# A gated FFT and token-MLP mixer: half-line tables with even samples first, ScalarE evictions that put the samples back in order, and x's first two row groups loaded whole

## The chip, the cores and the metric

The kernel runs on one core of one Trainium2 chip. The metric is device time in microseconds (us) of one execution; the median of several runs is compared. A profile is one execution taken by the hardware profiler; its span goes from the first to the last instruction. The engines are TensorE (PE, with its weight loads listed as PEld), VectorE (DVE), ScalarE (ACT), GpSimd (POOL) and SyncE (SP), which here only issues DMAs.

## The reference

Two mixers of the same shape are blended by a gate. S = 2048 tokens, D = 512 channels, F = 1792 hidden units; everything is bf16.

```python
def reference(A_x, A_w_r, A_w_i, B_x, B_w1, B_b1, B_w2, B_b2, gate_w):
    x = A_x
    g = sigmoid((x * gate_w).sum(-1, keepdims=True))
    # A: 2-D real FFT over (S, D), product with a complex W[S, 257], inverse
    X = rfft2(x, axes=(-2, -1)) * (A_w_r + 1j * A_w_i)
    a = irfft2(X, s=(S, D), axes=(-2, -1)).astype(bfloat16)
    # B: layer norm over D, then an MLP across the tokens
    h = layernorm(x)
    u = gelu(einsum("bsd,sf->bdf", h, B_w1) + B_b1)
    b = (einsum("bdf,fs->bds", u, B_w2) + B_b2).transpose(0, 2, 1)
    return g * a + (1 - g) * b
```

Both branches get the same x.

## The kernel before

**Tiling.** The 2048 rows of x are split as (q a r): q in 0..3, a in 0..127 on the partitions, r in 0..3. So there are 16 row groups j = 4q + r of 128 rows. Row group 0 is (q 0, r 0); the groups are loaded in the order of `Q0 = (0, 2, 1, 3)` for r = 0.

**The MLP branch.** The statistics of a row group are taken by DVE (L487, L488), for two groups by ACT (L491, L495); ACT takes a square root (L511), DVE the reciprocal (L516), and DVE (L521) or ACT (L527) writes the normalized `h`. The first product, `m1` (L705), is 14 blocks of F times 16 row groups: 224 matmuls of 512 columns. ACT applies the gelu (L721). The second product, `m2` (L1008), is another 224 matmuls of 512 columns; ACT evicts it scaled by 1 - g (L1014), for the last pair of row groups DVE does (L1021).

**The FFT branch.** It is done by butterflies on DVE and matmuls with tables of cosines and sines on PE:

- forward, along the tokens: a four-point butterfly on DVE (L535 to L542) for each r, then four matmul groups `fa` (L554 to L557) with table `ta`, each evicted by ACT (L560);
- a radix-4 step across the r (L585 to L601), then the transform along the channels, `fb` (L653, table `tb`, evicted at L660);
- the product with W: the mirrored half of W is made on PE by a matrix `flip` (L757; its last column, number 256, at L767 and L770); `wprep` (L777 to L781) scales row 0 of W by one half and takes sums and differences of columns 0 and 256; `nyq` (L801 to L804) does the line of the Nyquist frequency; `c0a`, `c0b`, `c0c` (L846) do column 0 apart;
- inverse along the tokens: `i1` (L890 for odd r, L895 to L898 for even r, table `ti`), evicted by `i1ev` (L904, L906), and DVE butterflies `zf` and `fq` (L914 to L927);
- inverse along the channels: `i3` (L967 to L970, table `tg`), evicted by ACT with the gate as scale at `i3ev` (L974), then DVE butterflies `es` (L987 to L993) and the sum of both branches (L1027).

The channels of a row are split by parity, h = 0 and 1; each half line has 256 time samples, and `i3` makes of the spectrum two parts: a part even in the sample number (129 values, by cosines) and a part odd in it (127 values, by sines). They stand side by side as 129 + 127 columns of one PSUM row. `es` then adds and subtracts them to get samples and mirrored samples. The terms of frequency 0 and of the line's last frequency share row 0 of the tables.

**The order of the work.** Nothing is scheduled by hand. Each piece is a task (`add`) with an engine, an estimated duration, what it reads and writes, a priority and the PSUM buffers it takes and frees. A small planner (`Plan.order`) simulates the engines with these durations and writes the tasks out in the order in which they start; `rate` gives it the speed of DMAs and `mm` the time of matmuls, with a least time of 120 columns. The order on each engine is then fixed. PSUM has four banks `acc`, two `fa` and two `fb`; during the first `m1` blocks one `fa` bank holds the output of block 0, so that one is left for the forward groups.

**The loads.** All loads go out on SP's queue but a few at the start: ACT's queue carries half of each of the first two row groups of x and the first two loads of w1. The halves are 64 partitions each (L366 to L370).

The functions that the change touches, with the line numbers of the profile:

Of the kernel before, what the change touches and what calls it, by code (L numbers as in the profile page):

```python
# [16 lines left out]
P = 128  # L17
# [17 lines left out]
def make_tables():  # L35
# [10 lines left out]
    for r in range(4):  # L46
        s = 4 * p + r
        for n, k0 in enumerate((0, 2)):
            th = ang(s, k0 + 4 * np.arange(64), S)
            ta[:, r, n * 128:n * 128 + 64] = np.cos(th)  # L50
            ta[:, r, n * 128 + 64:n * 128 + 128] = -np.sin(th)
        ta[:, r, 64] = alt
        th = ang(s, 1 + 4 * (p ^ 96), S)
        ta[:, r, 256:384] = np.cos(th)
        ta[:, r, 384:512] = -np.sin(th)
        ta[:, r, 512:640] = -np.cos(th)

        k = np.where(p < 64, 4 * p, 2 + 4 * (p - 64))
        o, w = ti_at(r)
        v = ti[:, o:o + w]  # L60
        if r % 2:
            sg = np.where(p < 64, 1.0, -1.0)[:, None]
            th = ang(k, s, S)
            v = v.reshape(P, 7, P)
            v[:, 0] = np.cos(th)
            v[:, 1] = sg * np.cos(th)
            v[:, 2] = -np.sin(th)
            v[:, 3] = -sg * np.sin(th)
            v[0, 2:4] = alt * (0.5 ** 0.5 if r == 1 else -(0.5 ** 0.5))
            th = ang(1 + 4 * (p ^ 96), s, S)  # L70
            v[:, 4] = -np.sin(th)
            v[:, 5] = np.cos(th)
            v[:, 6] = np.sin(th)
            ti[:, o:o + w] = v.reshape(P, w)
        else:
            s5 = np.append(s, 512)
            for lt, kk in enumerate((k, 1 + 4 * (p ^ 96))):
                th = ang(kk, s5, S)
                c, n = np.cos(th), -np.sin(th)
                if lt == 0:  # L80
                    n[0, 0:P] = 0.0 if r == 0 else -alt
                u = v[:, 256 * lt:256 * lt + 256]
                u[:, 0:P], u[:, P:] = c[:, 0:P], n[:, 0:P]
                if r == 0:
                    u[:, P] = c[:, P] if lt == 0 else -n[:, P]
    ti[:, 2945:3072] = ti[:, 129:256]
    ti[0, 2816:2945] = np.append(alt, 1.0)
# [12 lines left out]
    for r in range(4):  # L100
        cf[m[0, 0], r, 0] = 1.0
        cf[8, r, 0] = (1.0, -1.0)[r % 2]
        cf[m[1, r % 2], r, 0] = (1.0, -1.0, -1.0, 1.0)[r]
        if r != 2:
            cf[m[2, 0], r, 1], cf[m[3, 0], r, 1] = 1.0, (1.0, -1.0)[r % 2]
        if r != 0:
            cf[m[2, 1], r, 1], cf[m[3, 1], r, 1] = (0.0, -1.0, 1.0, 1.0)[r], (0.0, -1.0, -1.0, 1.0)[r]
    tb = np.concatenate([tb.reshape(P, 768), cf.reshape(P, 8)], 1)

    tg = np.zeros((P, 642))  # L110
    sc = 2.0 / (D * S)
    d = np.arange(129)
    for h in range(2):
        th = ang(2 * p + h, d, D)
        c, n = sc * np.cos(th), -sc * np.sin(th)
        if h == 0:
            c[0], n[0] = sc / 2, 0.0
            tg[:, 513:642], tg[:, 129:256] = c, n[:, 1:128]
        else:
            tg[:, 256:384], tg[:, 384], tg[:, 385:512] = c[:, 0:128], -n[:, 128], n[:, 1:128]  # L120
    tg[0, 0:129] = np.where(d % 2 == 0, 1.0, -1.0) * sc / 2
    return {"flip": bf(np.eye(P)[::-1]), "ta": bf(ta), "ti": bf(ti), "tb": bf(tb), "tg": bf(tg)}


def rate(at):
    return 260e3 if at < 8.4 else 388e3


class Task:
# [117 lines left out]
def d1(n):  # L247
    return 0.07 + n / 960.0
# [4 lines left out]


def mm(*ns):
    return sum(max(n, 120) / 2400.0 + 0.0025 for n in ns)

# [7 lines left out]
def kernel(  # L265
# [192 lines left out]
    def ld_ti():  # L458
        t["ti"] = sb([P, 3072], BF16, "rot")
        dma(t["ti"][:], tabs["ti"])  # L460
    load("tg", [P, 642], BF16, tabs["tg"], 164352, prio=39.5)


    def xe(r):
# [297 lines left out]
                add("ACT", act(512), wfe, reads=[("pw", comp, lt, a)], writes=[("W~", comp, lt)], prio=3, free=[tag])  # L762

    def wfn():
        pw = t["pwn"] = ps([P, 4, 2], F32, "fa", 2)
        for e in range(4):
            T.matmul(pw[:, e], lhsT=t["flip"][:], rhs=t["wt"][:, :, 3 - e, 256], start=True, stop=True)  # L767
    add("PE", mm(*[4] * 4), wfn, reads=[("wt", 0), ("wt", 1), "flip"], writes=["pwn"], prio=5, alloc=["fa"])
    wtk = [("W~", comp, 0) for comp in range(2)]
    add("ACT", 0.3, lambda: A.copy(t["W"][:, :, 0, :, 1, 256], t["pwn"][:].rearrange("p e k -> p k e")),  # L770
        reads=["pwn"], writes=wtk, prio=3, free=["fa"])
# [10 lines left out]
    add("DVE", 0.8, wprep, reads=[], writes=[("W", 0), ("W", 1), "wpm"] + wtk, prio=1)  # L782


    for lt in range(2):
# [8 lines left out]
        if lt == 0:  # L794
            def nyq():
# [77 lines left out]
    for rs, h in ((0, 0), (0, 1), (1, 0), (1, 1)):  # L873
        for r in (rs, rs + 2):
            for lt in range(2):
                tag = ("fa", "fb")[lt]

                def i1(h=h, r=r, lt=lt, tag=tag):
# [6 lines left out]
                    for v in range(2):  # L885
# [71 lines left out]
    for p in range(NJ // 2):  # L957
# [4 lines left out]
        def i3(j0=j0, j1=j1, rs=rs):  # L962
            g = t["tg"]
            for n, j in enumerate((j0, j1)):
                p3 = t["i3", j] = ps([P, 2, L], F32, ("fa", "fb")[n], 2)
                zv = [xph(h)[:, 2048 * rs:2048 * rs + 2048].rearrange("p (q v r a) -> p q v r a", q=4, v=2, r=2)[:, j // 4, :, n, :] for h in range(2)]
                T.matmul(p3[:, 0], lhsT=zv[0][:, 1], rhs=g[:, 0:256], start=True, stop=False)  # L967
                T.matmul(p3[:, 0, 0:129], lhsT=zv[0][:, 0], rhs=g[:, 513:642], start=False, stop=True)
                T.matmul(p3[:, 1, 0:128], lhsT=zv[1][:, 0], rhs=g[:, 256:384], start=True, stop=True)
                T.matmul(p3[:, 1, 128:256], lhsT=zv[1][:, 1], rhs=g[:, 384:512], start=True, stop=True)  # L970
        add("PE", mm(*[128] * 6, 256, 256), i3, reads=[("z", rs, 0), ("z", rs, 1), "tg"], writes=[("i3", j0), ("i3", j1)], prio=4, alloc=["fa", "fb"])
# [104 lines left out]
```

## Time and profile before

| | us |
|---|---|
| median of 3 runs | 127.93 (127.70 to 128.27) |
| the profiled execution | 128.01 |
| its span | 126.2 |
| PE busy | 121.4 (96%) |
| DVE busy | 114.4 (91%) |
| ACT busy | 81.0 (64%) |
| first matmul of `m1` starts | 5.74 |
| last eviction (L1021) starts | 123.46 |

How to read it: busy times of PE come from modelled ends, and records overlap; the distance from one start to the next is what a matmul costs. About 13 of the 756 matmuls have no record, each of which leaves a hole of 0.216 us. The first ten matmuls (L356) work on zeros and warm the clock; they start 0.427 us apart, the later ones of the same size 0.216.

### The profile page before, as it was taken

The page shows a single profiled execution, that of the slowest core. Times are in us where ns is not written, and L with a number is a line of the kernel's source. Part 1 is how long each engine was busy: PE and PEld are TensorE (multiplying, and loading weights), DVE is VectorE, ACT ScalarE, POOL GpSimd, SP SyncE. Part 2 cuts the span into 40 slices and gives each one's busy share as a digit, 9 for nine tenths or more (in the row PEclk, how much of TensorE's full clock was granted, in tenths as well). Part 3 has the DMA queues.
Part 4 walks back from the last instruction along what each step waited for, and adds up shares of the span by engine and source line. Part 5 has one row for each costly group of instructions (what it writes and reads, how often), then busy time and mean ns, then how long its engine had stood idle before and what let it go on. Part 6 is the DMA issues. An engine that isn't in the chain of part 4 may idle for free.

```text
span 126.2 us, 2141 instructions
## 1 busy us (share of the span) xinstructions
PE 121.4 (96%) x743; PEld 68.9 (55%) x756; DVE 114.4 (91%) x273; ACT 81.0 (64%) x165; POOL 0.2 (0%) x4
## 2 busy tenths in 40 slices
PE   6999999999999999999999999999999999999991
PEld 2244555555655466654455555555577767655590
DVE  2599999999999999999999999999988999999951
ACT  0972689699999999999520004732299999952200
POOL 0000000000000000000000000000000000000000
PEclk9999999999999999999999999999999999999999
DMA  2999999996367964599999940000000000021751
GB/s 63 266 368 363 379 363 362 349 330 89 99 124 225 275 133 112 125 393 412 413 408 409 407 173 0 0 5 0 3 0 0 0 5 0 0 82 58 280 208 44
DMA packets 18220, 23.12 MB, mean 183 GB/s; under 512 B 2191, under 2 KB 15905, under 8 KB 18209
## 3 DMA queue, kind: packets, MB, share of 16 engines
q1 hardware_dynamic: 17616, 22.36, 53.3%
q10 hardware_dynamic: 592, 0.62, 2.0%
q8 instruction: 6, 0.10, 0.3%
q14 instruction: 6, 0.04, 0.1%
HBM read 20.86 MB, written 2.10 MB: 182 GB/s over the span
## 4 chain that ended last, share of the span: by engine, by line
PE 93%; DMA 3%; ACTq 1%; issue 1%; DVE 0%
PE acc L1008 32%; PE acc L705 30%; PE fb L705 5%; PE fb L1008 5%; PE fa L705 3%; DMA wa<-in_B_w_dram 3%; PE fa L554 2%; PE fb L653 2%; PE fa L653 2%; PE fa L890 2%; PE fb L890 1%; PE fa L555 1%; ACTq L306 1%; PE fa L557 1%; PE fa L556 1%
## 5 line engine op out<-in xcount | busy, mean ns | idle before, releaser
L705 PE MATMUL acc<-h,wb 128*128 128x512 bf16 x108 | 25.9, 379 | 0.1
L1008 PE MATMUL acc<-gl,wb 128*128 128x512 bf16 (+1 forms) x94 | 24.0, 371 | 0.2
L1008 PE MATMUL acc<-gl,wa 128*128 128x512 bf16 (+1 forms) x97 | 23.8, 371 | 0.1
L1014 ACT ACTIVATE x<-acc,ombb,omg 128x512 bf16<-128x512 f32 x12 | 9.1, 782 | 21.2 <-PE acc L1008 21.2
L1008 PEld LDWEIGHTS <-wa 128*128 128x128 bf16 x126 | 13.5, 113 | 9.9
L1008 PEld LDWEIGHTS <-wb 128*128 128x128 bf16 x126 | 13.3, 113 | 9.3
L705 PE MATMUL acc<-h,wa 128*128 128x512 bf16 x62 | 17.5, 382 | 0.1
L705 PEld LDWEIGHTS <-wb 128*128 128x128 bf16 x112 | 10.7, 98 | 10.5
L705 PEld LDWEIGHTS <-wa 128*128 128x128 bf16 x112 | 10.3, 98 | 10.7 <-DMA wa<-in_B_w_dram 1.0
L487 DVE BATCH_NORM_STATS2 stats<-x 128x6 f32<-128x512 bf16 x14 | 9.5, 678 | 2.5 <-DMA x<-in_A_x_dram 2.5
L560 ACT CAST xp<-fa 128x512 bf16<-128x512 f32 x16 | 9.1, 582 | 2.0 <-PE fa L557 2.0
L735 ACT ACTIVATE x<-x 128x512 bf16<-128x512 bf16 x16 | 10.2, 691 | 0.0
L721 ACT ACTIVATE gl<-acc,b1f 128x512 bf16<-128x512 f32 x11 | 7.9, 718 | 3.2 <-PE acc L705 3.2
L705 PE MATMUL fb<-h,wa 128*128 128x512 bf16 x31 | 9.5, 379 | 0.1
L527 ACT ACTIVATE h<-x,nmr,rstd 128x512 bf16<-128x512 bf16 x11 | 8.4, 807 | 1.1 <-DMA wb<-in_B_w_dram 0.8
L705 PE MATMUL fa<-h,wa 128*128 128x512 bf16 x16 | 6.1, 393 | 0.1
L653 PEld LDWEIGHTS <-X 128*128 128x128 bf16 x64 | 4.7, 98 | 2.1
L974 ACT ACTIVATE B<-fb,g 128x512 bf16<-128x512 f32 x8 | 5.7, 713 | 0.0
L974 ACT ACTIVATE B<-fa,g 128x512 bf16<-128x512 f32 x8 | 5.6, 706 | 0.1
L356 PE MATMUL fa<-xp 128*128 128x512 bf16 x10 | 4.4, 631 | 1.2 <-DVE xp L317 1.2
L660 ACT CAST X<-fb 128x512 bf16<-128x512 f32 x8 | 5.1, 636 | 0.0
L511 ACT ACTIVATE rstd<-mv,eps 128x1 f32<-128x1 f32 (+1 forms) x11 | 3.2, 293 | 2.9 <-DVE mv L488 2.4
(169 smaller groups left out, 234.6 us busy)
## 6 DMA issues: line engine op xcount, KB each, us to landing
wb<-in_B_w_dram SPq DMA_DIRECT2D x11, 512.0 KB
wa<-in_B_w_dram SPq DMA_DIRECT2D x7, 512.0 KB
wa<-in_B_w_dram SPq DMA_DIRECT2D x2, 896.0 KB
wb<-in_B_w_dram SPq DMA_DIRECT2D x4, 384.0 KB
out_dram<-x SPq DMA_DIRECT2D x3, 512.0 KB
x<-in_A_x_dram SPq DMA_DIRECT2D x2, 512.0 KB
wa<-in_B_w_dram SPq DMA_DIRECT2D x2, 448.0 KB
rot<-dft_ti SPq DMA_DIRECT2D x1, 768.0 KB
```

The costliest lines, as they stand in the source:

```text
L356: T.matmul(pw[:], lhsT=t["warm"][:, 0:P], rhs=t["warm"], start=True, stop=True)
L487: V.bn_stats(out=t["stats"][:, j, :], in_=t["x"][:, j // 4, j % 4, :])
L527: add("ACT", 0.71, lambda j=j: A.activation(t["h"][:, j // 4, j % 4, :], t["x"][:, j // 4, j % 4, :], ActF.Identity, bias=t["nmr"][:, j:j ...
L560: add("ACT", act(512), lambda r=r, dq=dq: A.copy(xe(r)[:, :, :, dq, :], t["pa", r, dq][:]), reads=[("pa", r, dq)], writes=[("X", r, dq)], ...
L653: T.matmul(pb[:, k % 2, k // 2], lhsT=t["X"][:, lt, EX[e], c, k, :], rhs=tbl(k, c), start=True, stop=True)
L660: A.copy(t["X"][:, lt, EX[e]].rearrange("p c j l -> p (c j l)").rearrange("p (h c g b) -> p h c g b", h=2, c=2, b=2)[:, :, c], t["pb", lt, ...
L705: T.matmul(t["u", ft][:], lhsT=w[:, j // 4, j % 4, c * P:(c + 1) * P], rhs=t["h"][:, j // 4, j % 4, :], start=(j == jorder[0]), stop=(j == ...
L721: gelus.append(add("ACT", act(512, 1) , lambda ft=ft: A.activation(t["gl"][:, ft, :], t["u", ft][:], ActF.Gelu_apprx_tanh, bias=t["b1f"][: ...
L735: A.activation(t["x"][:, q, r, :], t["x"][:, q, r, :], ActF.Copy, accum_out=t["glog"][:, 4 * q + r:4 * q + r + 1])
L974: A.activation(eo_v(p)[:, n], t["i3", j][:], ActF.Copy, scale=t["g"][:, j:j + 1])
L1008: T.matmul(t["y", j, m][:, cs], lhsT=w[:, o, 512 * q + r:512 * q + 512:4], rhs=t["gl"][:, ft, cs], start=(ft == 0), stop=(ft == NFT - 1))
L1014: A.activation(tbuf(j).rearrange("p h d -> p (h d)"), t["y", j, 0][:], ActF.Identity, bias=t["ombb2"][:, j:j + 1], scale=t["omg"][:, j:j + 1])
```

## The change

Five edits in one.

1. **Tables and matmuls of `i3`, and of `i1` for r = 0, lt = 0.** The columns of the half-line tables are sorted by the parity of the sample number, even ones first. The cosine of a frequency and of its complement agree at even samples and differ in sign at odd ones, and so the row that the two end frequencies share is arranged anew: instead of one matmul of 256 columns and one of 129, there are three of 191, 64 and 65 columns. The second input half (`zv[1]`) keeps two matmuls of 128 columns, each now written as two runs of 64.
2. **The evictions put the samples back in order.** `i3ev` and, for r = 0 and lt = 0, `i1ev` read PSUM in order and write SBUF with a step of two elements. What follows on DVE is unchanged.
3. **Sums and differences of the end columns.** With the shared row holding sum and difference of the two end frequencies, the scaling of row 0 of W goes (its factors move to the tables), `c0c` adds and subtracts in place of a copy, `nyq` gets an addition and a subtraction, and a table for the lines on partition 0 is changed to match.
4. **The flip of column 256** is one matmul of 8 columns in place of four of 2.
5. **Loads and costs.** Row groups (q 0, r 0) and (q 2, r 0) of x are loaded whole, the first on SP's queue, the second on ACT's. The planner's DMA rate at the start goes from 260 to 275 KB/us and the least time of a matmul from 120 to 62 columns; the costs of the changed tasks follow.

The order which the planner writes is therefore another one in places. On SP and ACT one DMA is gone at the start; the four groups `fa` of r = 0 stand after 24, 28, 32 and 38 matmuls of `m1` (before: 25, 28, 32 and 37).

```diff
 def rate(at):
-    return 260e3 if at < 8.4 else 388e3
+    return 275e3 if at < 8.4 else 388e3
...
 def mm(*ns):
-    return sum(max(n, 120) / 2400.0 + 0.0025 for n in ns)
+    return sum(max(n, 62) / 2400.0 + 0.0025 for n in ns)
...
     for q in (0, 2):
-        for n in range(2):
-            hp = slice(n * P // 2, (n + 1) * P // 2)
-            ld([("xh", q, n)], lambda hp=hp, q=q: t["x"][hp, q, 0, :], x4[hp, q, 0, :], 65536, -9.5 + 0.1 * q, ("SP", "ACT")[n])
-        add("DVE", 0.0, lambda: None, reads=[("xh", q, 0), ("xh", q, 1)], writes=[("x", 0, q)], prio=-9)
+        ld([("x", 0, q)], lambda q=q: t["x"][:, q, 0, :], x4[:, q, 0, :], 131072, -9.5 + 0.1 * q, "ACT" if q else "SP")
...
-        pw = t["pwn"] = ps([P, 4, 2], F32, "fa", 2)
-        for e in range(4):
-            T.matmul(pw[:, e], lhsT=t["flip"][:], rhs=t["wt"][:, :, 3 - e, 256], start=True, stop=True)
+        pw = t["pwn"] = ps([P, 2, 4], F32, "fa", 2)
+        T.matmul(pw[:], lhsT=t["flip"][:], rhs=t["wt"][:, :, :, 256], start=True, stop=True)
...
-        V.tensor_scalar_mul(W[0:1, :, 0, 0, :, 0:257], W[0:1, :, 0, 0, :, 0:257], 0.5)
...
-                V.tensor_mul(nn[:, :, 0], t["c0"][0:1, 0, 0, 1, :], wn[:, 0, 0:257:256])
+                V.tensor_mul(pz[:, 0:2], t["c0"][0:1, 0, 0, 1, :], wn[:, 0, 0:257:256])
+                V.tensor_add(nn[:, 0, 0:1], pz[:, 0:1], pz[:, 1:2])
+                V.tensor_sub(nn[:, 1, 0:1], pz[:, 0:1], pz[:, 1:2])
...
-            V.tensor_copy(t["B"][:, lt, :, :, 0], t["ce"][:, lt].rearrange("p e c k -> p e (c k)"))
+            b, ce = t["B"][:, lt], t["ce"][:, lt]
+            V.tensor_add(b[:, :, 0:4:2, 0], ce[:, :, :, 0], ce[:, :, :, 1])
+            V.tensor_sub(b[:, :, 1:4:2, 0], ce[:, :, :, 0], ce[:, :, :, 1])
...
-                            if n > P:
-                                T.matmul(p1[:, v], lhsT=d(1), rhs=t["ti"][:, 2816:3072], start=True, stop=False)
...
+                            if r == 0 and lt == 0:
+                                T.matmul(p1[:, v, 65:256], lhsT=d(1), rhs=t["ti"][:, 2816:3007], start=True, stop=False)
+                                T.matmul(p1[:, v, 128:192], lhsT=d(0), rhs=u[:, 66:130], start=False, stop=True)
+                                T.matmul(p1[:, v, 0:65], lhsT=d(0), rhs=u[:, 0:65], start=True, stop=True)
...
-                        A.copy(t["ze"][:, h, r // 2, lt], t["i1", h, r, lt][:])
+                        o, i = t["ze"][:, h, r // 2, lt], t["i1", h, r, lt][:]
+                        if r == 0 and lt == 0:
+                            o, i = o.rearrange("p v (n w) -> p v w n", w=2), i.rearrange("p v (w n) -> p v w n", w=2)
+                        A.copy(o, i)
...
-                T.matmul(p3[:, 0], lhsT=zv[0][:, 1], rhs=g[:, 0:256], start=True, stop=False)
-                T.matmul(p3[:, 0, 0:129], lhsT=zv[0][:, 0], rhs=g[:, 513:642], start=False, stop=True)
-                T.matmul(p3[:, 1, 0:128], lhsT=zv[1][:, 0], rhs=g[:, 256:384], start=True, stop=True)
-                T.matmul(p3[:, 1, 128:256], lhsT=zv[1][:, 1], rhs=g[:, 384:512], start=True, stop=True)
+                ph = p3[:, 1].rearrange("p (w n) -> p w n", w=2)
+                gh = g[:, 322:578].rearrange("p (c w n) -> p c w n", c=2, w=2)
+                T.matmul(p3[:, 0, 65:256], lhsT=zv[0][:, 1], rhs=g[:, 0:191], start=True, stop=False)
+                T.matmul(p3[:, 0, 128:192], lhsT=zv[0][:, 0], rhs=g[:, 258:322], start=False, stop=True)
+                T.matmul(p3[:, 0, 0:65], lhsT=zv[0][:, 0], rhs=g[:, 192:257], start=True, stop=True)
+                for c in range(2):
+                    T.matmul(ph[:, :, 64 * c:64 * c + 64], lhsT=zv[1][:, c], rhs=gh[:, c], start=True, stop=True)
...
-                A.activation(eo_v(p)[:, n], t["i3", j][:], ActF.Copy, scale=t["g"][:, j:j + 1])
+                A.activation(eo_v(p)[:, n].rearrange("p h (n w) -> p h w n", w=2), t["i3", j][:].rearrange("p h (w n) -> p h w n", w=2), ActF.Copy, scale=t["g"][:, j:j + 1])
```

More of the change, by code (lines that the diff above doesn't have):

```diff
@@ L83, in make_tables @@
                 u[:, 0:P], u[:, P:] = c[:, 0:P], n[:, 0:P]
[L84 to L87, printed above, removed]
+                if r == 0 and lt:
+                    u[:, P] = -n[:, P]
+                elif r == 0:
+                    ti[:, 2816:2879], ti[:, 2943:3007] = n[:, 2:P:2], n[:, 1:P:2]
+                    u[:, 0:65], u[:, 66:130] = c[:, 0:129:2], c[:, 1:P:2]
+                    u[0, 66:130], ti[0, 2879:2943] = 0.0, 1.0
     tb = np.zeros((P, 2, 2, 3, 64))
@@ L107, in make_tables @@
             cf[m[2, 1], r, 1], cf[m[3, 1], r, 1] = (0.0, -1.0, 1.0, 1.0)[r], (0.0, -1.0, -1.0, 1.0)[r]
+    cf[:, 0] = cf[:, 0] @ np.array([[1.0, 1.0], [1.0, -1.0]])
+    cf[0:2] *= 0.5
     tb = np.concatenate([tb.reshape(P, 768), cf.reshape(P, 8)], 1)
-    tg = np.zeros((P, 642))
+    tg = np.zeros((P, 578))
     sc = 2.0 / (D * S)
@@ L116, in make_tables @@
         if h == 0:
-            c[0], n[0] = sc / 2, 0.0
-            tg[:, 513:642], tg[:, 129:256] = c, n[:, 1:128]
-        else:
-            tg[:, 256:384], tg[:, 384], tg[:, 385:512] = c[:, 0:128], -n[:, 128], n[:, 1:128]
-    tg[0, 0:129] = np.where(d % 2 == 0, 1.0, -1.0) * sc / 2
+            tg[:, 0:63], tg[:, 127:191] = n[:, 2:128:2], n[:, 1:128:2]
+            tg[:, 192:257], tg[:, 258:322] = c[:, 0:129:2], c[:, 1:128:2]
+            tg[0] = 0.0
+            tg[0, 63:127] = tg[0, 192:257] = sc / 2
+        else:
+            tg[:, 322:386], tg[:, 386:450] = c[:, 0:128:2], c[:, 1:128:2]
+            tg[:, 450], tg[:, 451:514], tg[:, 514:578] = -n[:, 128], n[:, 2:128:2], n[:, 1:128:2]
     return {"flip": bf(np.eye(P)[::-1]), "ta": bf(ta), "ti": bf(ti), "tb": bf(tb), "tg": bf(tg)}
 def rate(at):
-    return 260e3 if at < 8.4 else 388e3
+    return 275e3 if at < 8.4 else 388e3
 class Task:
@@ L460, in ld_ti @@
         dma(t["ti"][:], tabs["ti"])
-    load("tg", [P, 642], BF16, tabs["tg"], 164352, prio=39.5)
+    load("tg", [P, 578], BF16, tabs["tg"], 147968, prio=39.5)
     def xe(r):
@@ L764, in wfn @@
     def wfn():
-        pw = t["pwn"] = ps([P, 4, 2], F32, "fa", 2)
-        for e in range(4):
-            T.matmul(pw[:, e], lhsT=t["flip"][:], rhs=t["wt"][:, :, 3 - e, 256], start=True, stop=True)
-    add("PE", mm(*[4] * 4), wfn, reads=[("wt", 0), ("wt", 1), "flip"], writes=["pwn"], prio=5, alloc=["fa"])
+        pw = t["pwn"] = ps([P, 2, 4], F32, "fa", 2)
+        T.matmul(pw[:], lhsT=t["flip"][:], rhs=t["wt"][:, :, :, 256], start=True, stop=True)
+    add("PE", mm(8), wfn, reads=[("wt", 0), ("wt", 1), "flip"], writes=["pwn"], prio=5, alloc=["fa"])
     wtk = [("W~", comp, 0) for comp in range(2)]
-    add("ACT", 0.3, lambda: A.copy(t["W"][:, :, 0, :, 1, 256], t["pwn"][:].rearrange("p e k -> p k e")),
+    add("ACT", 0.3, lambda: A.copy(t["W"][:, :, 0, :, 1, 256], t["pwn"][:, :, ::-1]),
         reads=["pwn"], writes=wtk, prio=3, free=["fa"])
@@ L781, in wprep @@
         V.tensor_sub(pv[1], ends[1][:, :, 0], ends[1][:, :, 1])
-    add("DVE", 0.8, wprep, reads=[], writes=[("W", 0), ("W", 1), "wpm"] + wtk, prio=1)
+    add("DVE", 0.4, wprep, reads=[], writes=[("W", 0), ("W", 1), "wpm"] + wtk, prio=1)
     for lt in range(2):
@@ L803, in nyq @@
                 V.tensor_add(nn[:, 1], na[:, 1, 1], na[:, 0, 0])
-                V.tensor_mul(nn[:, :, 0], t["c0"][0:1, 0, 0, 1, :], wn[:, 0, 0:257:256])
-            add("DVE", 3 * d1(512) + 0.1, nyq, reads=[("B", i, e) for i in range(2) for e in range(4)] + [("W", 0), ("W", 1), ("c0", 0)] + pbk, writes=["nn"], prio=0.5)
+                V.tensor_mul(pz[:, 0:2], t["c0"][0:1, 0, 0, 1, :], wn[:, 0, 0:257:256])
+                V.tensor_add(nn[:, 0, 0:1], pz[:, 0:1], pz[:, 1:2])
+                V.tensor_sub(nn[:, 1, 0:1], pz[:, 0:1], pz[:, 1:2])
+            add("DVE", 3 * d1(512) + 0.35, nyq, reads=[("B", i, e) for i in range(2) for e in range(4)] + [("W", 0), ("W", 1), ("c0", 0)] + pbk, writes=["nn"], prio=0.5)
         def c0b(lt=lt):
@@ L845, in c0c @@
         def c0c(lt=lt):
-            V.tensor_copy(t["B"][:, lt, :, :, 0], t["ce"][:, lt].rearrange("p e c k -> p e (c k)"))
-        add("DVE", 0.15, c0c, reads=[("ce", lt)], writes=bk, prio=pr)
+            b, ce = t["B"][:, lt], t["ce"][:, lt]
+            V.tensor_add(b[:, :, 0:4:2, 0], ce[:, :, :, 0], ce[:, :, :, 1])
+            V.tensor_sub(b[:, :, 1:4:2, 0], ce[:, :, :, 0], ce[:, :, :, 1])
+        add("DVE", 0.3, c0c, reads=[("ce", lt)], writes=bk, prio=pr)
         if lt == 0:
@@ L891, in i1 @@
                         else:
-                            n = 129 if r == 0 and lt == 0 else P
                             u = ti[:, 256 * lt:256 * lt + 256]
-                            if n > P:
-                                T.matmul(p1[:, v], lhsT=d(1), rhs=t["ti"][:, 2816:3072], start=True, stop=False)
-                            else:
-                                T.matmul(p1[:, v, n:], lhsT=d(1), rhs=u[:, n:], start=True, stop=True)
-                            T.matmul(p1[:, v, 0:n], lhsT=d(0), rhs=u[:, 0:n], start=(n == P), stop=True)
-                i1t[h, r, lt] = add("PE", mm(*([256] * 4 if r % 2 else [128] * 4)), i1, reads=[("T", lt, r % 2), "ti"] + ([("T", lt, 1)] if r == 2 else []), writes=[("i1", h, r, lt)], prio=3, alloc=[tag])
+                            if r == 0 and lt == 0:
+                                T.matmul(p1[:, v, 65:256], lhsT=d(1), rhs=t["ti"][:, 2816:3007], start=True, stop=False)
+                                T.matmul(p1[:, v, 128:192], lhsT=d(0), rhs=u[:, 66:130], start=False, stop=True)
+                                T.matmul(p1[:, v, 0:65], lhsT=d(0), rhs=u[:, 0:65], start=True, stop=True)
+                            else:
+                                T.matmul(p1[:, v, P:], lhsT=d(1), rhs=u[:, P:], start=True, stop=True)
+                                T.matmul(p1[:, v, 0:P], lhsT=d(0), rhs=u[:, 0:P], start=True, stop=True)
+                i1t[h, r, lt] = add("PE", mm(*([256] * 4 if r % 2 else [128] * 4 if r or lt else [191, 64, 65] * 2)), i1, reads=[("T", lt, r % 2), "ti"] + ([("T", lt, 1)] if r == 2 else []), writes=[("i1", h, r, lt)], prio=3, alloc=[tag])
                 def i1ev(h=h, r=r, lt=lt):
@@ L966, in i3 @@
                 zv = [xph(h)[:, 2048 * rs:2048 * rs + 2048].rearrange("p (q v r a) -> p q v r a", q=4, v=2, r=2)[:, j // 4, :, n, :] for h in range(2)]
[L967 to L971, printed above, removed]
+                ph = p3[:, 1].rearrange("p (w n) -> p w n", w=2)
[5 more added lines that the diff above has]
+                    T.matmul(ph[:, :, 64 * c:64 * c + 64], lhsT=zv[1][:, c], rhs=gh[:, c], start=True, stop=True)
+        add("PE", mm(*[191, 64, 65, 128, 128] * 2), i3, reads=[("z", rs, 0), ("z", rs, 1), "tg"], writes=[("i3", j0), ("i3", j1)], prio=4, alloc=["fa", "fb"])
         for n, j in enumerate((j0, j1)):
             def i3ev(j=j, n=n, p=p):
-                A.activation(eo_v(p)[:, n], t["i3", j][:], ActF.Copy, scale=t["g"][:, j:j + 1])
+                A.activation(eo_v(p)[:, n].rearrange("p h (n w) -> p h w n", w=2), t["i3", j][:].rearrange("p h (w n) -> p h w n", w=2), ActF.Copy, scale=t["g"][:, j:j + 1])
             add("ACT", act(512, 1), i3ev, reads=[("i3", j), "g"] + ([("eo", j0)] if n else []), writes=[("eo", j)], prio=1.5, free=[("fa", "fb")[n]],
```

## The prediction

> **What bounds the kernel now.** I read the page's first two parts, then its chain of waits, then the timeline of the first 8 us and of the stage of the last transform. Busy shares and slices of TensorE (PE):
>
> ```profile
> PE 121.4 (96%) x743; PEld 68.9 (55%) x756; DVE 114.4 (91%) x273; ACT 81.0 (64%) x165; POOL 0.2 (0%) x4
> PE   6999999999999999999999999999999999999991
> PE 93%; DMA 3%; ACTq 1%; issue 1%; DVE 0%
> ```
>
> The reader should see that PE has no hole and that 93% of the chain is PE. So the end is: when PE starts its real work, plus the sum of its matmuls, plus a tail. The chain in order of time over the first 6 us, then lines of the timeline there:
>
> ```profile
> 0.73 0.56 ACTq L306
> 1.32 0.61 ACTq L306
> 1.97 3.73 DMA wa<-in_B_w_dram
> 5.74 0.61 PE fa L705
> ...
> 3.42 0.69 DVE L487 BATCH_NORM_STATS2 stats<-x 128x6 f32<-128x512 bf16 x1 [1.92 <-DMA x<-in_A_x_dram]
> 4.38 0.29 ACT L361 ACTIVATE ombb<-eps 128x1 f32<-128x1 f32 x1
> 4.58 0.28 ACT L511 ACTIVATE rstd<-mv,eps 128x1 f32<-128x1 f32 x1
> 5.09 0.41 DVE L521 TENSOR_SCALAR h<-x,mv,rstd 128x512 bf16<-128x512 bf16 x1
> ```
>
> PE's first real matmul, at 5.74, waits for a load of w1 that ACT could issue only after its two half loads of x. The other operand, h, is ready at 5.50, only 0.24 before. So there are two starts to beat. The timeline in the last transform (start, duration, line) and at the flip of the weights' last column:
>
> ```profile
> 99.95 0.27 PE L967 MATMUL fa<-tg,xp 128*128 128x256 bf16 x1
> 100.06 0.22 PE L968 MATMUL fa<-tg,xp 128*128 128x129 bf16 x1
> 100.12 0.22 PE L969 MATMUL fa<-tg,xp 128*128 128x128 bf16 x1
> 100.18 0.22 PE L970 MATMUL fa<-tg,xp 128*128 128x128 bf16 x1
> 100.23 0.27 PE L967 MATMUL fb<-tg,xp 128*128 128x256 bf16 x1
> ...
> 53.99 0.24 PE L767 MATMUL fa<-wt,flip 128*128 128x2 bf16 x4
> 54.10 0.59 PE L705 MATMUL acc<-h,wb 128*128 128x512 bf16 x2
> ```
>
> The durations overlap, so what a matmul costs is the distance to the next start: 0.109 us for 256 columns, 0.057 for 129, 0.056 for 128. That is columns/2.4 ns plus about 2.5. Four matmuls of 2 columns, each with its own weight load, take 54.10 - 53.99 = 0.11, 0.027 each: the floor of a pair of weight load and matmul.
>
> **The change part by part.** *Matmuls of the last transform (i3).* Per row group, 256 + 129 columns (0.166) become 191 + 64 + 65. By columns/2.4 + 2.5 ns these are 0.082 + 0.029 + 0.030 = 0.141, and the short two are just above the floor of 0.027. The other two keep 128 columns. 0.025 saved, 16 times: -0.40. PE is the chain here, so it passes to the end.
>
> *Matmuls of the first inverse stage (i1), r = 0 and lt = 0.* The same trade, four times: -0.10.
>
> *The flip of column 256.* Four matmuls become one of 8 columns: three times 0.027, -0.08. PE work in all: -0.57 (0.574).
>
> A rule speaks against it. The Trainium skill (TensorE: Matmul & The Clock Gate, "Back-to-back issue gap") says that a stream of weight-load and matmul pairs sustains some 81 ns a matmul at 128 columns and 131 at 512. Estimated from it, 256 + 129 would be 98 + 81 = 179 ns and the three new ones 89 + 81 + 81 = 251, which over 20 groups is 1.4 us more: 129.4 instead of 127.3. The trace shows 56 ns at 128 columns and 216 at 512, so I go by the trace; the mechanism is rival D.
>
> *Order on PE.* The list written by the planner changes, since short matmuls are now costed shorter. Of real stalls the timeline shows two: 0.19 at 12.5, where the second forward group waits for ACT to clear the only free buffer, and 0.14 at 17.1, where an h is late. In the changed order the first forward group stands one matmul earlier, so the first stall (0.19) goes. But the fourth stands one matmul later, and ACT normalizes the late h behind that group's eviction. So the h is late at the same 17.2 while PE arrives 0.19 earlier: the second stall grows to 0.33. I count 0; bounds -0.33 (both gone) to +0.2 (one such wait more).
>
> *x's loads.* ACT issues one load of x in place of two, so w1's first load goes out 0.61 earlier: at its flight of 3.73 PE could start at 5.13. Then h binds. Row group 0 came as two halves of 64 KB on two queues (issued at 0.72 and 0.73, used at 3.42); now it is 128 KB on SP, with 128 KB for group 2 on ACT beside it. No row shows that. Lower bound of the delay: 0, if the flight is latency. Upper: 128 KB more ahead of its last byte at the 192 GB/s that the window 2.5 to 3.5 shows, 0.68. The window 4.5 to 5.5 runs at 344 GB/s, 0.38; the loads share, so not all of it lies ahead: I take 0.3. Statistics then end at 4.63 instead of 4.33. The square root waited before for ACT (table load 3.08 to 4.36, then a dummy square root at 4.38), which is now 0.6 earlier, so it starts at 4.66 instead of 4.58, and h ends at 5.58. PE starts at 5.63: -0.11. The first matmuls run slowly (starts 0.40 and 0.42 apart, then 0.216 from 6.57 on), so an early start is worth half: -0.06. The second group's h was ready at 7.48 for a matmul at 7.66; it moves by the same +0.08, the matmul by -0.11, and with the semaphore's way some 0.03 is lost. Net -0.03. Bounds: -0.2 (no delay: start 5.35) and +0.15 (start 6.0). The loads behind come earlier on both queues: SP issues one fewer, 0.6. Nothing on the chain waits for those, since PE shows no other wait on a DMA.
>
> *VectorE (DVE).* The scaling of row 0 of W goes (57.77 to the next start at 58.22: -0.45). Two copies become two pairs of small operations (0.09 more each) and the Nyquist line gains two (0.08 to 0.12 each). Net about -0.07, hidden anyway: DVE is done at 120.18 and waits 0.18 for PE's next accumulator, then 0.78, 0.30 and 0.43. If PE comes 0.6 earlier, the first wait turns into 0.4 of DVE being late, which the 1.5 of later waits absorbs; that cover is gone beyond about 1 us.
>
> *ScalarE (ACT).* 16 evictions of i3 and two of i1 write every second element. No row has such a write. Below: no cost (a gain is excluded: as many elements as before). The nearest rows are the evictions at L660, which read PSUM with strides (every pair of elements from places 128 apart): they start 0.475 apart, as do the contiguous ones at L904 (96.27, 96.75). Above: twice the element time, 0.43 more on the 0.57 between starts of L974. I take 0, by L660. The Trainium skill (SBUF — State Buffer, "Door 1: The DMA port swizzle") says that strides inside a 16-byte line are free, up to 8 bf16; no row here shows that for a write. It sets no term.
>
> *The rest.* 16 KB less of table: nothing, it lands long before use.
>
> **Sum.** The profiled execution took 128.01, its span 126.2; it lies 0.08 above the median of the three runs, 127.93. -0.40 - 0.10 - 0.08 - 0.03 is -0.6: 127.4 for that execution, 127.3 against the median.
>
> **The rivals.** *B, the saving is eaten at the start.* Group 0's load shares the queues with w1's first load, now 0.6 earlier, and flies as long as that does (3.73 instead of 2.70). For it: the window 3.5 to 4.5 moves only 112 GB/s, so something there is slow. Against it: x is issued first. Then statistics start at 4.45, the square root at 5.39, h ends at 6.31 and PE starts at 6.35, 0.61 late, of which one slow matmul fewer gives back 0.19; the second group's h, at 8.29 for a matmul at 8.05, costs 0.25. +0.67 - 0.57: 128.0.
>
> *C, the other side: the strided write is slow on ACT.* Between 100 and 111 ACT runs evictions nearly end to end (0.57 apart). PE can run pair 7 of i3 at 109.2 only when the fa buffer of pair 5 is cleared, and that happens at 108.52: 0.7 of slack behind some 12 evictions. So up to 0.06 more per eviction costs nothing; each further 0.1 costs 1.2 us. From 0.16 on, the run is over 0.5% slower than before. At twice the element time: 12 x 0.43 - 0.7 = 4.5 lost, less 0.57: 131.8. Against it only L660, whose stride is on the read.
>
> *D, weight loads bind the short matmuls.* Each weight load has a record of 98 ns. If a pair can't be shorter, a group goes from 0.166 to 0.294, 20 times: +2.6, 130.5. Against it: pairs start 0.056 and 0.027 apart today.
>
> **How the numbers follow.** Forecast 0.60, B 0.24, C 0.11, D 0.05. The forecast's own range is 126.8 (both stalls gone, start at its best: 127.93 - 0.57 - 0.33 - 0.2) to 127.6 (0.15 and 0.2 lost). The whole range goes up to 128.8, which is C at 0.18 per eviction: beyond lie D and most of C, below 126.8 little. 0.5% is 0.64 us and about what a measurement of this kernel can tell from no change: faster means below 127.29, which the forecast's sum just misses and two thirds of its range lie below: 0.40. Same: the rest of the forecast and most of B, 0.40. Slower: C, D and a little of B, 0.20.
>
> **What would show it.** Starts in i3: 0.082, 0.029, 0.030 apart (D: 0.1). L974's successor 0.57 apart (C: 0.65 or more, and PE waiting for ACT between 102 and 110). First real matmul at 5.6 with h ending just before (B: over 6.0). The wait at 12.5 gone, the one at 17.1 doubled. What would make it wrong: a wait of PE in the middle that the old order did not have.

## The result, and the profile after

The changed kernel takes 128.10 us (median; 127.77 to 128.53) beside 127.84 us of the kernel before in the same runs (127.67 to 128.27). The ratio is 1.0021, with an interval of 1.0013 to 1.0030: 0.2% slower, where 0.5% faster was forecast. The profiled execution took 128.40 us with a span of 126.6 (before: 128.01 and 126.2).

Busy time, slices of TensorE and shares of the chain in the page of the changed kernel:

```profile
PE 122.1 (96%) x773; PEld 69.0 (54%) x773; DVE 114.3 (90%) x276; ACT 83.0 (66%) x165; POOL 0.2 (0%) x4
PE   6999999999999999999999999999999999999990
PE 88%; ACT 8%; issue 1%; DVE 1%
```

The slices hardly differ from before. The chain does: PE has fallen from 93% to 88%, and ACT, which had no share of its own, has 8%. Where that lies is in the chain in order of time (start, us, what). The stretch of the last transform:

```profile
100.47 1.22 ACT B L986 x2
101.86 0.75 ACT x L1026
...
103.19 4.26 ACT B L986 x6
107.45 0.62 ACT x L1026
108.07 2.12 ACT B L986 x3
110.65 11.46 PE acc L1020 x60
```

From 100.5 to 110.2 the chain runs through ACT's evictions of i3 (L986, which was L974 before), and only then returns to PE. The costliest groups give the length of one such eviction, first in the page of before, then in that of after (busy us, mean ns of one, idle before):

```profile
L974 ACT ACTIVATE B<-fb,g 128x512 bf16<-128x512 f32 x8 | 5.7, 713 | 0.0
L974 ACT ACTIVATE B<-fa,g 128x512 bf16<-128x512 f32 x8 | 5.6, 706 | 0.1
```

```profile
L986 ACT ACTIVATE B<-fa,g 128x512 bf16<-128x512 f32 x8 | 7.1, 886 | 0.1
L986 ACT ACTIVATE B<-fb,g 128x512 bf16<-128x512 f32 x8 | 7.1, 888 | 0.0
```

The same elements now take 887 ns in place of 710. The records of neighbours overlap, so the price is the distance between starts. It is 0.675 on average where it was 0.57: 0.105 us more for each eviction. ACT's timeline of before, then of the changed kernel:

```profile
103.39 0.71 ACT L974 ACTIVATE B<-fa,g 128x512 bf16<-128x512 f32 x1
103.96 0.72 ACT L974 ACTIVATE B<-fb,g 128x512 bf16<-128x512 f32 x1
```

```profile
103.19 0.83 ACT L986 ACTIVATE B<-fb,g 128x512 bf16<-128x512 f32 x1
103.86 0.85 ACT L986 ACTIVATE B<-fa,g 128x512 bf16<-128x512 f32 x1
```

What that does to PE is in PE's timeline, first for a row group at the beginning of i3 and then for one in the middle:

```profile
100.01 0.25 PE L978 MATMUL fa<-tg,xp 128*128 128x191 bf16 x1
100.09 0.19 PE L979 MATMUL fa<-tg,xp 128*128 128x64 bf16 x1
100.12 0.20 PE L980 MATMUL fa<-tg,xp 128*128 128x65 bf16 x1
100.16 0.27 PE L982 MATMUL fa<-tg,xp 128*128 128x128 bf16 x2
100.27 0.24 PE L978 MATMUL fb<-tg,xp 128*128 128x191 bf16 x1
...
108.51 0.27 PE L982 MATMUL fa<-tg,xp 128*128 128x128 bf16 x2
108.86 0.24 PE L978 MATMUL fb<-tg,xp 128*128 128x191 bf16 x1
```

At 100 the two matmuls of L982 are followed after 0.11 by the other half of the pair. At 108.51 it takes 0.35: PE stands for 0.23, until ACT has cleared the `fb` bank. There are four such waits in i3 (0.11, 0.21, 0.23 and 0.23, at 105.3, 106.6, 108.6 and 110.0; together 0.78) and two in i1, whose two evictions with the same write are late in the same way (0.12 and 0.10, at 92.1 and 93.4). The trace of before has none of them; its last pair of i3:

```profile
109.47 0.22 PE L970 MATMUL fa<-tg,xp 128*128 128x128 bf16 x1
109.53 0.27 PE L967 MATMUL fb<-tg,xp 128*128 128x256 bf16 x1
```

The start of the chain, and the timeline around it:

```profile
1.21 4.45 PE fa L362 x10
...
0.73 1.34 SPq L312 DMA_DIRECT2D x<-in_A_x_dram  x3
0.73 0.40 ACTq L312 DMA_DIRECT2D x<-in_A_x_dram  x1
3.12 0.69 DVE L490 BATCH_NORM_STATS2 stats<-x 128x6 f32<-128x512 bf16 x1 [1.62 <-DMA x<-in_A_x_dram]
...
4.60 0.41 DVE L524 TENSOR_SCALAR h<-x,mv,rstd 128x512 bf16<-128x512 bf16 x1
5.46 0.63 PE L708 MATMUL fa<-h,wa 128*128 128x512 bf16 x1
```

Row group 0 is used at 3.12, 0.30 earlier than before (3.42), h ends at 5.01 in place of 5.50, and w1 is there too. PE's first real matmul, at 5.46, now waits for neither: it follows the ten warming matmuls (L362). It is 0.28 earlier than before. In both traces the first two real matmuls are slow (0.40 to 0.43 from one start to the next), and the sixth, at `fb`, starts at 6.98 where it started at 7.22: worth 0.24 between these two executions.

The other waits of PE are in the forward stage. The one at 12.5 is gone. The later one:

```profile
16.56 0.22 PE L560 MATMUL fa<-rot,gl 128*128 128x128 bf16 x1
16.98 0.38 PE L708 MATMUL fa<-h,wa 128*128 128x512 bf16 x1 [0.19 <-ACT h L530]
```

L708 would follow 0.06 after the last matmul of L560 and starts 0.42 after it: 0.355 of wait, for an h that ACT normalizes behind the eviction of a forward group.

**The sum on PE**, after less before: start -0.24, forward waits +0.02 (0.355 in place of 0.19 + 0.14), PE's work -0.57, waits in i1 +0.22, waits in i3 +0.78. That is +0.21. DVE's last sum, which closes the chain, starts at 123.71 where it started at 123.46: +0.25. The medians differ by +0.26. The two profiled executions differ by +0.39; the other 0.14 lies behind that last sum. The start is the part of the sum that one execution each can't fix: when PE passes from 0.427 to 0.216 between starts is not the same in every execution (shown below, under the attempts on what is left), so that the sum meets the medians within 0.05 is partly luck.

### The profile page after: what moved, and what is told of

Same layout as the page of the kernel before. It is cut to its first block, busy times and chain, and to the rows that moved or that the text cites. A ratio compares the mean times of both kernels' runs of the same rounds, so it can differ in the third digit from the quotient of the medians.

```text
span 126.6 us, 2185 instructions
## 1 busy us (share of the span) xinstructions
PE 122.1 (96%) x773; PEld 69.0 (54%) x773; DVE 114.3 (90%) x276; ACT 83.0 (66%) x165; POOL 0.2 (0%) x4
## 4 chain that ended last, share of the span: by engine, by line
PE 88%; ACT 8%; issue 1%; DVE 1%
PE acc L708 30%; PE acc L1020 28%; ACT B L986 6%; PE fb L1020 5%; PE fb L708 5%; PE fa L362 4%; PE fa L708 3%; PE fa L895 1%; PE fb L656 1%; PE fa L656 1%; PE fb L895 1%; PE fa L558 1%; PE fa L557 1%; ACT x L1026 1%; PE fa L560 1%
## 5 line engine op out<-in xcount | busy, mean ns | idle before, releaser
L708 PE MATMUL acc<-h,wb 128*128 128x512 bf16 x112 | 27.0, 379 | 0.0
L708 PE MATMUL acc<-h,wa 128*128 128x512 bf16 x64 | 17.8, 383 | 0.0
L708 PEld LDWEIGHTS <-wb 128*128 128x128 bf16 x112 | 10.7, 98 | 10.6
L708 PEld LDWEIGHTS <-wa 128*128 128x128 bf16 x112 | 10.5, 99 | 10.4 <-issue 1.1
L708 PE MATMUL fb<-h,wa 128*128 128x512 bf16 x32 | 9.7, 379 | 0.0
L986 ACT ACTIVATE B<-fa,g 128x512 bf16<-128x512 f32 x8 | 7.1, 886 | 0.1
L986 ACT ACTIVATE B<-fb,g 128x512 bf16<-128x512 f32 x8 | 7.1, 888 | 0.0
L708 PE MATMUL fa<-h,wa 128*128 128x512 bf16 x16 | 6.2, 395 | 0.2 <-ACT h L530 0.2
L362 PE MATMUL fa<-xp 128*128 128x512 bf16 x10 | 4.5, 632 | 1.2 <-DVE xp L323 1.2
```

Of the source, the lines that this page charges most:

```text
L362: T.matmul(pw[:], lhsT=t["warm"][:, 0:P], rhs=t["warm"], start=True, stop=True)
L708: T.matmul(t["u", ft][:], lhsT=w[:, j // 4, j % 4, c * P:(c + 1) * P], rhs=t["h"][:, j // 4, j % 4, :], start=(j == jorder[0]), stop=(j == ...
L986: A.activation(eo_v(p)[:, n].rearrange("p h (n w) -> p h w n", w=2), t["i3", j][:].rearrange("p h (w n) -> p h w n", w=2), ActF.Copy, scal ...
```

## The experiments

In these the kernel before, in the same runs, had a median of 127.78, 127.72 or 127.92 us, and each ratio is taken against it.

### The stride on the read instead of the write

The changed kernel, with the order of the loops in the two evictions turned: ACT walks PSUM in steps of 128 values and writes SBUF in order. Everything else, the order of all instructions too, is as in the changed kernel.

```diff
-o, i = o.rearrange("p v (n w) -> p v w n", w=2), i.rearrange("p v (w n) -> p v w n", w=2)
+o, i = o.rearrange("p v (n w) -> p v n w", w=2), i.rearrange("p v (w n) -> p v n w", w=2)
...
-A.activation(eo_v(p)[:, n].rearrange("p h (n w) -> p h w n", w=2), t["i3", j][:].rearrange("p h (w n) -> p h w n", w=2), ...)
+A.activation(eo_v(p)[:, n].rearrange("p h (n w) -> p h n w", w=2), t["i3", j][:].rearrange("p h (w n) -> p h n w", w=2), ...)
```

> The changed kernel with the step of two moved from the write to the read: the evictions of the last transform and of the first inverse stage write SBUF in order and read PSUM at places 128 elements apart. The order on PE is that of the changed kernel. Theory (the strided write is what eats the saving): evictions start 0.57 us apart instead of 0.675, PE's four waits in the last transform (0.78 us in all) and its two in the first inverse stage (0.22) go, and the time is 128.1 - 1.0 = 127.1, 0.994 of before. Rival 1 (the new order is at fault: pairs of the last transform stand too close for any eviction): waits stay, 128.0. Rival 2 (a strided read costs as much as a strided write): evictions stay 0.67 apart, 128.1.

Measured: 126.99 us (126.89 to 127.28), ratio 0.9929 (0.9906 to 0.9951). ACT's and PE's timelines of this kernel:

```profile
102.55 0.68 ACT L986 ACTIVATE B<-fb,g 128x512 bf16<-128x512 f32 x1
103.12 0.69 ACT L986 ACTIVATE B<-fa,g 128x512 bf16<-128x512 f32 x1
...
107.83 0.27 PE L982 MATMUL fa<-tg,xp 128*128 128x128 bf16 x2
107.94 0.24 PE L978 MATMUL fb<-tg,xp 128*128 128x191 bf16 x1
```

Evictions start 0.57 apart again, and the `fb` half follows the `fa` half after 0.11: no wait of PE is left in i1 or i3. The same permutation of the same elements is free on the read and costs 0.105 on the write. It is worth 1.1 us between these two kernels, for 1.0 of waits (0.78 + 0.22). Against the kernel before, -0.79 agrees with what is left of the sum above: PE's work (-0.57) and the start (-0.24). This version beats both kernels.

### The strided write alone, in the kernel before

Only the sixteen evictions of i3 write every second element. The matmuls, the loads and the order of the kernel before stay. The samples come out of order, so the output is permuted.

```diff
-A.activation(eo_v(p)[:, n], t["i3", j][:], ...)
+A.activation(eo_v(p)[:, n].rearrange("p h (n w) -> p h w n", w=2), t["i3", j][:].rearrange("p h (w n) -> p h w n", w=2), ...)
```

> The kernel before, in which only the 16 evictions of the last transform write with a step of two (the samples of a half line then stand permuted, so the output differs; nothing is left out). It prices the strided write on the old order, where the pairs of the last transform stand where they did. Theory: 0.105 us more per eviction; by the prediction's own sum 12 x 0.105 - 0.7 = 0.56 of waiting on PE: 128.3 to 128.5. Rival (the new order's closer pairs were needed for the waits): 127.8, unchanged.

Measured: 128.54 us (128.52 to 128.86), ratio 1.0066 (1.0053 to 1.0080), 0.82 us more. ACT's timeline, and PE's at one of the waits:

```profile
104.18 0.86 ACT L974 ACTIVATE B<-fb,g 128x512 bf16<-128x512 f32 x1
104.85 0.87 ACT L974 ACTIVATE B<-fa,g 128x512 bf16<-128x512 f32 x1
...
107.60 0.22 PE L970 MATMUL fa<-tg,xp 128*128 128x128 bf16 x1
107.82 0.27 PE L967 MATMUL fb<-tg,xp 128*128 128x256 bf16 x1
```

Again 0.675 apart, and PE waits four times in i3 (0.14, 0.16, 0.17 and 0.19, at 104.9, 106.2, 107.6 and 109.6): 0.66 together; the other 0.16 of the medians is not placed. So the write is enough by itself, and neither the new matmul shapes nor the new order is needed for it. In the changed kernel the same waits are 0.12 longer in all; that its shorter matmuls bring PE to each pair a little earlier, or that its pairs stand elsewhere among the matmuls of `m2`, would fit that, but no run takes it apart.

### The planner told of the dearer eviction

The changed kernel, strided write kept, with 0.105 us more in the planner's estimate of the eighteen evictions.

```diff
-add("ACT", act(512), i1ev, ...
+add("ACT", act(512) + (0.105 if r == 0 and lt == 0 else 0), i1ev, ...
...
-add("ACT", act(512, 1), i3ev, ...
+add("ACT", act(512, 1) + 0.105, i3ev, ...
```

> The changed kernel as it is, but the planner is told that an eviction with a strided write takes 0.105 us longer; it puts up to six more of the second product's matmuls between the pairs of the last transform. Theory: the evictions stay 0.675 apart, PE fills the time instead of waiting, and most of the 1.0 us comes back: 127.2 to 127.4. Rival 1 (the order as such is at fault, not the price): no better, 128.0 or more. A third way: the pairs come so late that DVE ends after PE at the tail; then 127.6 to 128.

Measured: 127.00 us (126.91 to 127.50), ratio 0.9933 (0.9907 to 0.9959). ACT's timeline, and PE's where one pair ends and the next begins:

```profile
103.18 0.84 ACT L986 ACTIVATE B<-fa,g 128x512 bf16<-128x512 f32 x1
103.85 0.86 ACT L986 ACTIVATE B<-fb,g 128x512 bf16<-128x512 f32 x1
...
105.17 0.27 PE L982 MATMUL fa<-tg,xp 128*128 128x128 bf16 x2
105.29 0.24 PE L978 MATMUL fb<-tg,xp 128*128 128x191 bf16 x1
```

The evictions are as slow as in the changed kernel, and still PE doesn't wait: the planner now sets the pairs of i3 further apart. The first two of the eight pairs stand together, with 362 matmuls of the MLP ahead of them in both kernels; ahead of the other six there are 368, 375, 379, 386, 390 and 394, in the changed kernel 367, 373, 376, 379, 385 and 388. In i1 a group in an `fb` bank now stands between the two groups with the strided write, and the waits there are gone too. So the price of the strided write is not lost by its nature. What cost time was a list of instructions written for an eviction of 0.57, with an eviction of 0.675 in it.

### What a strided write costs

In the kernel with the strided read, eighteen copies of 128x512 bf16 from SBUF into a scratch buffer behind the last eviction: three each with steps of 1, 2, 4 and 8 bf16, then three each with steps of 1 and 2 float32. They are extra work, so the kernel's own time (142.37) means nothing.

```diff
+for k in (1, 2, 4, 8):
+    for _ in range(3):
+        A.activation(v(st[:, 0:512 * k:k]), v(src), ActF.Copy, scale=t["g"][:, 0:1])
+f = st[:].bitcast(F32)
+for k in (1, 2):
+    for _ in range(3):
+        A.activation(v(f[:, 0:512 * k:k]), v(src), ActF.Copy, scale=t["g"][:, 0:1])
```

> The kernel with the strided read, and behind ACT's last eviction 18 copies of one 128x512 bf16 tile from SBUF to scratch, three each: bf16 written with steps of 1, 2, 4 and 8 elements, then float32 with steps 1 and 2. They are extra work and make the span longer; what counts is the distance between their starts. Theory 1 (a step breaks pairs of bf16 that are else written together): steps 2, 4 and 8 all cost about 0.1 us more than step 1, float32 in order too or not at all. Theory 2 (the price is by the bytes spanned): step 4 costs more than step 2, step 8 more still. Rival, by the Trainium skill's 16-byte lines (SBUF - State Buffer): steps up to 8 bf16 are free, and the 0.105 comes from something else in the eviction.

ACT's timeline at the first copy of step 1, the last of step 8 and the first of float32:

```profile
117.08 0.71 ACT L1059 ACTIVATE st<-gl,g 128x512 bf16<-128x512 bf16 x1
...
131.66 2.56 ACT L1059 ACTIVATE st<-gl,g 128x512 bf16<-128x512 bf16 x1
134.25 0.72 ACT L1063 ACTIVATE st<-gl,g 128x512 f32<-128x512 bf16 x1
```

The durations are 0.72 us for step 1 in bf16, 0.89 for step 2, 1.43 for step 4 and 2.56 for step 8; in float32 0.72 for step 1 and 0.75 for step 2. So the price of a bf16 write grows with its step, which refutes theory 1. The Trainium skill (SBUF — State Buffer, "Door 1: The DMA port swizzle") counts strides inside a 16-byte line, up to 8 bf16, as free; here these steps cost 0.17, 0.71 and 1.84 us, so the measurement decides against it for ScalarE's writes. Bytes alone don't set the price either: elements 8 bytes apart cost 0.03 in float32 (step 2) and 0.71 in bf16 (step 4), against theory 2. This is one execution, with three copies of each kind that agree within 0.02. The mechanism stays open.

### The loads of x in halves again

Once in the changed kernel and once in the one with the strided read, with the edit undone that loads two row groups whole.

```diff
-ld([("x", 0, q)], lambda q=q: t["x"][:, q, 0, :], x4[:, q, 0, :], 131072, -9.5 + 0.1 * q, "ACT" if q else "SP")
+for n in range(2):
+    hp = slice(n * P // 2, (n + 1) * P // 2)
+    ld([("xh", q, n)], lambda hp=hp, q=q: t["x"][hp, q, 0, :], x4[hp, q, 0, :], 65536, -9.5 + 0.1 * q, ("SP", "ACT")[n])
+add("DVE", 0.0, lambda: None, reads=[("xh", q, 0), ("xh", q, 1)], writes=[("x", 0, q)], prio=-9)
```

In the changed kernel:

> The changed kernel with x's first two row groups again as two halves each; the order on PE is the same. Theory: the first real matmul starts at 5.74 again instead of 5.46, of which half a slow matmul is given back, so 0.24 is lost: 128.35. Rival (the earlier start is swallowed by a later wait): 128.1.

Measured: 128.25 us (128.17 to 129.47), ratio 1.0037 (1.0012 to 1.0062). PE starts at 5.56 and then waits 0.28 at 6.85 for the second group's h. In the kernel with the strided read:

> The kernel with the strided read, with x's first two row groups again as two halves each: the shorter matmuls and the new order without the change of the loads. Theory: 0.15 to 0.25 us more than with whole loads (128.25 against 128.10 between the two kernels with the strided write): 127.2. Rival (with PE no longer waiting for ACT, the start is worth its full 0.3 us): 127.3. A second rival (the loads give nothing and the 0.15 was scatter): 127.0.

Measured: 127.50 us (127.19 to 128.26), ratio 0.9981 (0.9963 to 0.9998). PE's timeline:

```profile
6.65 0.59 PE L711 MATMUL fb<-h,wa 128*128 128x512 bf16 x2
7.66 0.38 PE L711 MATMUL fa<-h,wa 128*128 128x512 bf16 x1 [0.42 <-DVE h L527]
```

Two matmuls at 0.21 would end their turn at 7.08; the next starts at 7.66, 0.58 late, and waits for the second group's h. So the whole loads are worth 0.15 us by the medians in the changed kernel, where the intervals of the two ratios overlap, and 0.5 in the one whose later waits are gone, where they don't. What they save there is less the first matmul than the second group's h. Both are earlier in every profile of this record: the first group's h ends at 4.96 to 5.14 in the six with whole loads and at 5.50 to 5.52 in the five with halves, the second group's at 6.75 to 6.93 and at 7.29 to 7.61.

### The order alone

The kernel before with the two numbers of the planner that the change sets, and nothing else: its matmuls and loads are the old ones.

```diff
-    return 260e3 if at < 8.4 else 388e3
+    return 275e3 if at < 8.4 else 388e3
...
-    return sum(max(n, 120) / 2400.0 + 0.0025 for n in ns)
+    return sum(max(n, 62) / 2400.0 + 0.0025 for n in ns)
```

> The kernel before with the planner's two numbers of the change alone (275 for the early DMA rate, a least matmul of 62 columns): the forward groups stand after 24, 28, 32, 38 matmuls, the rest of the list is as before. Theory from the prediction: the wait of 0.19 us at 12.5 goes, the one of 0.14 at 17.1 grows to 0.33, time unchanged, 127.84 within 0.1. Rival: the new order costs a wait of its own, 128.0 or more.

Measured: 128.01 us (127.71 to 128.36), ratio 1.0006 (0.9989 to 1.0023): no difference that can be told from none. In its profile the later wait is 0.35 as in the changed kernel. At 12.5 there is still a wait, of 0.54, but now for a load of w1:

```profile
12.48 0.22 PE L557 MATMUL fa<-rot,gl 128*128 128x128 bf16 x1
13.07 0.39 PE L705 MATMUL fa<-h,wa 128*128 128x512 bf16 x1 [0.38 <-DMA wa<-in_B_w_dram]
```

The changed kernel has no such wait, nor have the two with halves above, so halves of x alone don't explain it; the cause stays open.

### Two attempts on what is left

Both start from the kernel with the strided read. The first takes away one of the ten warming matmuls, so that PE can start when h is ready.

```diff
-    NWARM = 10
+    NWARM = 9
```

> The kernel with the strided read and 9 in place of 10 warming matmuls. In the changed kernel the tenth ends at 5.46, where the first real matmul starts, while h and w1 are ready at about 5.0. Theory: the start comes 0.3 us earlier, but the second group's h is ready only at about 7.0 and PE waits there, so at most 0.2 is won: 126.8 to 127.0. Rival (the start is the bound, in full): 126.65.

Measured: 127.08 us (126.93 to 127.57), ratio 0.9951 (0.9934 to 0.9969): no gain on 126.99. PE's timeline:

```profile
5.03 0.63 PE L708 MATMUL fa<-h,wa 128*128 128x512 bf16 x1
5.46 1.84 PE L708 MATMUL acc<-h,wa 128*128 128x512 bf16 x4
7.13 0.60 PE L708 MATMUL fb<-h,wa 128*128 128x512 bf16 x2
```

Real work begins 0.42 earlier, but the first five real matmuls start 0.42 apart on average, so the sixth (at `fb`) starts at 7.13; in the profile of the kernel with the strided read it starts at 6.84. From there the distance is 0.22. Neither theory had that: in this execution PE has no hole for the second group's h to explain, and it is the slow matmuls that take the gain.

Other executions need not be like it. PE passes from 0.43 to 0.22 between starts at about 7.1 here, at 6.2 in the profile of the kernel with the strided read, and at 4.9 in that of the kernel whose planner knows the price, which has the same instructions up to there and all ten warming matmuls:

```profile
1.21 4.02 PE L362 MATMUL fa<-xp 128*128 128x512 bf16 x10 [1.21 <-DVE xp L323]
...
6.23 0.59 PE L708 MATMUL fb<-h,wa 128*128 128x512 bf16 x2
6.94 0.38 PE L708 MATMUL fa<-h,wa 128*128 128x512 bf16 x1
```

There the sixth real matmul starts at 6.23, and the eighth 0.28 late, when the second group's h is ready (6.89), as the theory had it. By the medians the kernels with nine and with ten warming matmuls are equal; why they are, one profile of each doesn't show.

The second sets the planner's rate for early DMAs back to 260, which puts the forward groups elsewhere.

```diff
-    return 275e3 if at < 8.4 else 388e3
+    return 260e3 if at < 8.4 else 388e3
```

> The kernel with the strided read, and the planner's early DMA rate back at 260: the forward groups then stand after 26, 30, 34, 38 matmuls of the first product, one or two later than with 275 but for the fourth. In the kernel with the strided read PE waits 0.355 us at 16.4 for an h that ACT normalizes behind the fourth forward group's eviction. Theory: the fourth group stands where it stood, so this wait stays, and the time is 126.9 to 127.1. Rival (the wait depends on how the first three groups delay ACT, and goes when they are spread): 126.65.

Measured: 127.04 us (126.89 to 127.36), ratio 0.9927 (0.9901 to 0.9952), the same as with 275. The wait of 0.355 at 16.4 is gone from its trace, but the time isn't shorter. Three matmuls at the start of that execution ran slowly for 0.26 more in all than in the other's trace, which hides most of the gain in the profiles. The medians are equal as well, and where the 0.35 went in the other executions stays open.

## Why the prediction was wrong

**The step that failed: ScalarE's strided write at 0, by L660.** L660 reads PSUM with strides and writes in order. The prediction took its price for a stride on the write, and noted itself that no row had such a write. The read was indeed free: the first experiment has it at 0.57. The write costs 0.105 per eviction. This is rival C at a small price, and its own sign was there: starts 0.65 apart or more, and PE waiting for ACT between 102 and 110. "A gain is excluded" was right; the value should have stood between the ends, not at the lower one, as the nearest row was one of another kind of access.

**The formula of rival C was nearly right.** 12 x 0.105 - 0.7 gives 0.56; the waits in i3 came to 0.78, in the old kernel with the write alone to 0.66. It left out i1, where two evictions cost 0.22 more. With that the rival's own terms give 0.78 lost against 0.6 won: 0.2 slower, which is what was measured, but by luck: the waits came to 1.00 in all and the rest of the change won 0.79, and the two misses of 0.2 cancel. Its break-even against the saving, 0.11 per eviction by the same formula (0.57 + 0.7 over 12), sat right at the price that was then found. So the sign hung on a number that no row of the trace held, and a chance of 0.11 was too low for it.

**x's loads.** The prediction had group 0 land 0.3 later, with "no delay" as the best case. It was used 0.30 earlier. The lower bound excluded a gain without a reason. Rows that spoke for a gain were at hand: in the trace of before the issue of the two halves on ACT took 0.56 and 0.61, that of a whole load of x on SP, at 2.89, 0.42. In the changed kernel the whole load on ACT took 0.40. PE started at 5.46, not 5.63, bounded by the warming matmuls, which the prediction didn't look at. The term was -0.24 instead of -0.03. That an early start is worth half did not hold either: 0.28 earlier gave 0.24 between these two executions, and the moment when PE becomes fast, on which it hangs, differs from one execution to the next. Rival B (PE at 6.35) is refuted.

**Right.** The matmuls: starts in i3 are 0.08, 0.03 and 0.03 apart, and a group takes 0.256 in place of 0.28 (-0.40 in all); rival D is refuted. The clean kernel gains 0.79 for -0.57 and -0.24, so PE's work came through whole where nothing ate it. The order: the wait at 12.5 is gone and the later one is 0.355, with 0.33 forecast; the order alone cost nothing measurable. DVE stayed hidden: it waits for PE 0.3 or more before each of its last four sums. In the kernel with the strided read, where PE does come earlier, the first of these waits is gone and the other three (0.65, 0.30, 0.43) remain, as forecast.

**The whole sum again, with what was measured**: -0.57 (work) - 0.24 (start) + 0.02 (forward waits) + 0.22 (i1) + 0.78 (i3) = +0.21, where -0.6 was forecast. What would make it wrong was named, too: a wait of PE in the middle that the old order did not have.

## What to carry to other kernels

A stride on the read and the same stride on the write are two prices; where one instruction permutes, put the jumps on the side that a row of the trace shows to be free, and where no row shows it, measure it before an order is built on it. An engine that runs end to end between a producer and its buffer passes each 0.1 us on to the producer once the slack is used, however low its busy share (ACT: 66%). And when an order is written from estimates, a changed instruction needs its new estimate: 0.105 us told to the planner was worth as much here as making the instruction fast again.

## What the runs showed of the hardware

- ScalarE's bf16 writes cost more with their step: 0.72, 0.89, 1.43 and 2.56 us for 128x512 at steps of 1, 2, 4 and 8. In an eviction from PSUM, step 2 adds 0.105 to 0.57 between starts; a read of PSUM in pairs of values 128 apart adds nothing.
- The first matmuls of 512 columns start 0.427 apart and the later ones 0.216, and the moment of the change differs between executions: about 4.9, 6.2 and 7.1 us in three profiles with the same ten warming matmuls or nine of them. The granted clock in the profile's rows doesn't show it: it is 1.00 from 1.5 to 6.5 us in the trace of before, where the starts are still 0.40 to 0.43 apart. A single profile therefore can't price an edit of the start.
- One load of 128 partitions was issued faster than one of its halves (0.40 us against 0.56 and 0.61 on ACT's queue), and row group 0, loaded whole on SP's queue, was used 0.30 us earlier.
